# Rounded halves of q and k placed by ScalarE or VectorE, and rows of maxima issued from ScalarE's queue, in a clustered-attention and mixture-of-experts kernel

## The chip, the cores and the metric

One core of one Trainium2 chip runs the whole kernel in one launch. The metric is the device time in microseconds of one execution. A profile is one execution taken by the hardware profiler; its times count from the start of its span.

## The reference

Attention over 4 batches of 8 heads, 768 positions, 64 dimensions. Every query and key is assigned to the nearest of 16 centroids, and a query sees only keys of its own cluster. The result then goes through a routed layer of 8 experts with at most 80 tokens each.

```python
q_assign = np.argmax(np.einsum('bhsd,hcd->bhsc', q_n, c_n), axis=-1)
k_assign = np.argmax(np.einsum('bhsd,hcd->bhsc', k_n, c_n), axis=-1)
mask = q_assign[:, :, :, None] == k_assign[:, :, None, :]
scores = np.where(mask, scale * np.matmul(q, k.transpose(0, 1, 3, 2)), -1000000000.0)
scores = scores - np.max(scores, axis=-1, keepdims=True)
attn = np.exp(scores)
attn = attn / (np.sum(attn, axis=-1, keepdims=True) + 1e-09)
x = np.matmul(attn, v)                        # then merged over heads to 3072 x 512
logits = x @ w_gate                           # top-1 of 8 experts, the 80 largest gates each
out[tok] = gate[tok, None] * (np.maximum(x[tok] @ w1[e], 0.0) @ w2[e])
```

## The kernel before

The 32 heads are worked in 16 pairs. Each head has six units of 128 keys, and a pair has twelve. For each unit TensorE computes two score tiles of 128 x 384 (lines 470 and 471, two matmuls each), ScalarE takes their exponentials (line 476), GpSimd adds them up (line 485), and TensorE multiplies them by the values (line 494).

q and k are split into a rounded half "hi" (type fp32r) and the rest "lo". A head's operands lie in two tiles, QAB and KAB, of 128 partitions x 2 slots x 768; there are six of each, used in turn. Slot 0 holds hi, 16 rows of one-hot cluster numbers and, in QAB, one row with the negative of each query's maximum; slot 1 holds hi and lo stacked. `pair` fills them: ScalarE rounds k and q into a tile `hi` (lines 269 and 295), GpSimd subtracts to get lo (lines 271 and 301), and DMAs on SyncE's queue (SP) carry the parts into place, all through `copy`, so that they all carry line 80 in the profile. KAB gets four DMAs of hi, QAB two that write both slots at once, and each head gets two one-hot DMAs (`oh`) for KAB and two for QAB. Masked q (line 291) needs the one-hot tile and a matmul (line 289) first.

One pair ahead of the scores, the maxima pass runs on slot 0 alone: a matmul (line 433) into one of two PSUM tiles `sm`, and a VectorE maximum over it (line 435). After a head's twelve maxima, `shift` reduces them, TensorE turns them (line 453), ScalarE rounds them into `row` (line 456), and a DMA of 3 KB writes them as one row of QAB. Line 471 cannot run for that head before this row has landed; line 433 cannot run before hi and the one-hot rows are in place. Score tiles have three PSUM buffers.

The order of all instructions is made by a planner (class `Flow`): steps carry an engine, a duration, what they need and a due time `at`, and the planner emits the step that can start first on its engine, in the order of due times among those nearly ready. The table `CFG` holds the due times. Every engine and every DMA queue then runs its own list in that order, so a step that waits holds up all behind it on its engine. A DMA uses one of eight semaphores in turn and waits until the DMA eight places ahead of it in the program has landed, whichever queue that one is on.

After the pairs come the logits, the choice of tokens, and eight experts (lines 1014 and 1042).

Of the kernel before, what the change touches and what calls it, by code (L numbers as in the profile page):

```python
# [7 lines left out]
F32 = mybir.dt.float32  # L8
# [11 lines left out]
CFG = dict(at=dict(sum=-2.92, av=6.36, xT=11.45, lt=5.48, turn=6.25, sm=1.07, exp=-3.24, mx=-0.64), stick=1.99, wait=0.06,  # L20
           idle=0.25, dummy=128, bias=0.67, side=(-1.86, 0.07), prep=(-0.18, 0.32), lead=(-40.37, -29.82, -36.45, -34.77, -18.44),
           zero=(-15.23, 0.59, -7.6, 0.13), start=dict(pe=6.1, act=4.8, dve=7.5, pool=2.5, dma=0.0), warm=48, cold=38.0, lag=0.8,
           hold=dict(dve=(0.08, -0.06), act=(0.67, 0.23), pe=(0.25, 0.02)), nab=6, pps=9, sums=8, xts=4, vs=2, skew=3, raws=4,
           lds=3, keys=1, adds=6, weigh=(8, 5.0, 4.5), slots=(16, 8), native1=(), native2=(0, 1, 2, 3, 4, 5), early=((2, 6),
           185.8), scaled=(), spread=(), mix=dict(ld=-22.86, st=-21.43, hi1=-7.61, lo1=-8.07, hi2=-7.72, lo2=2.21, xg=-34.18,
           xp=-9.37, out=11.74, sc=-9.18, a0=4, a1=2, a2=5, spare=0.3))
# [10 lines left out]
BOTH = ("dve", "pool")  # L37


class Program:  # L40
# [160 lines left out]
    def assign(self, b, p):  # L201
# [34 lines left out]
        yield Step("act", .58, also=("dve", .75), needs=[("hi", "q", *divmod(r - 2, self.NP))] if r > 2 else [])  # L236
# [14 lines left out]
    def pair(self, b, p):  # L251
# [9 lines left out]

        yield Step("none", 0.0, needs=[("ld", "k", b, p)])
# [4 lines left out]
        for f in range(2):  # L267
            yield Step("act", .5)
            nc.scalar.copy(hi[:, f * HS:(f + 1) * HS], t[:, f * HS:(f + 1) * HS])  # L269
# [9 lines left out]
        yield Step("none", 0.0, needs=[("oh", b, p)], key=("hi", "k", b, p), dma=[.1] * 4)  # L279
        onehot("k", self.KAB)  # L280
        yield Step("none", 0.0, needs=[("ld", "q", b, p), ("oh", b, p)])
# [10 lines left out]
        for f in range(2):  # L292
            fs = slice(f * HS, (f + 1) * HS)
            yield Step("act", .5)
            nc.scalar.copy(hi[:, fs], t[:, fs])  # L295
# [116 lines left out]
    def ready(self, b, h, full):  # L412

        p = h // 2
        if b or p:
            return [("full" if full else "hi", n, b, p) for n in "kq"]
        return [["k0l", "q0l", "full0"], ["k1l", "q1l", "q1h", "k1h", "oh1", ("hi", 1)]][h] if full else [[("hi", 0)], ["k1h", "oh1", ("hi", 1)]][h]
# [19 lines left out]
    def shift(self, b, h):  # L437
# [68 lines left out]
    def turns(self, r):  # L506
# [4 lines left out]
        for f in range(2):  # L511
# [4 lines left out]
            yield Step("act", .48, alt=("dve", .55), give="misc", key=("turn", r, f), dma=[1.1])  # L516
# [697 lines left out]
    def prologue(self, flow):  # L1214
# [11 lines left out]
        for p in range(CFG["lds"]):  # L1226
            for n in "kq":
                dma(("ld", n, 0, p), 1.09, self.load, 0, p, n)
# [21 lines left out]
        for r in range(CFG["vs"] - 1):  # L1250
            dma(("ldv", r), 1.09, self.load_v, r)
# [5 lines left out]
    def stream(self, flow):  # L1257
# [10 lines left out]
        def loads(n):  # L1268

            for r in range(CFG["lds"], R):  # L1270
                yield Step("dma", 1.09, needs=self.taken(n, *divmod(r - CFG["lds"], NP)), key=("ld", n, *divmod(r, NP)))
                self.load(*divmod(r, NP), n)

        def vs():
            for r in range(CFG["vs"] - 1, R):
                yield Step("dma", 1.09, needs=[("av", r - CFG["vs"], NC - 1), ("span", r - CFG["vs"])] if r >= CFG["vs"] else [], key=("ldv", r))
                self.load_v(r)

        def begin(t):
# [19 lines left out]
            if k in (4, 10) and 2 * r + k // 6 < self.NT:  # L1299
                i = 2 * r + k // 6  # L1300
                flow.dma(flow.now, .73)
# [29 lines left out]
        def weighs():  # L1331
            N1, K1 = self.w1.shape[1] // P, E * self.w1.shape[1] // P
            for n in range(K1):
                u = CFG["weigh"][0] + int(CFG["weigh"][1] * n)
                e, k = divmod(n, N1)
                yield Step("dma", 1.46, key=("wl", n), late=CFG["weigh"][2], needs=[("st", units[u][0] * NC + units[u][1], 0)] + [("wm", n - 1)] * (n > 0), at=u)
# [120 lines left out]
def Step(eng, t, **more):  # L1457

    return SimpleNamespace(**{**dict(eng=eng, t=t, key=None, needs=(), at=None, late=0.0, rows=.5, early=False, alt=None, also=None, dma=(), take=None, give=None, kind=0, room=None, seq=False, swdge=0.0, port=(), made=None, bar=None, even=False), **more})
# [38 lines left out]
class Flow:  # L1498
# [5 lines left out]
    def __init__(self, free):  # L1504
        self.free, self.end, self.lanes, self.lock = dict(free), {}, [], {}
        self.now, self.kind, self.queue, self.work, self.origin, self.port = 0.0, 0, 0.0, {0: 3000.0, 1: 3100.0}, 0.0, 0.0
        self.idle, self.filled, self.first, self.ahead = None, 0, None, 1e9

# [50 lines left out]
    def run(self):  # L1559
        while True:  # L1560
# [52 lines left out]
            done = start + t  # L1613
# [100 lines left out]
```

## Time and profile before

| | |
|---|---|
| three runs | median 605.52 us, 604.53 to 613.6 |
| the profiled execution | 609.25 us |
| its span, first to last instruction | 607.1 us |
| TensorE busy (matmuls) | 566.0 us, 93% |
| VectorE, GpSimd, ScalarE busy | 416.1, 393.5, 331.3 us |
| mean granted TensorE clock | 0.951 |
| DMA | 124.47 MB, mean 205 GB/s |

The pairs take the span up to about 486 us, the choice of tokens up to about 519 us, the experts the rest. Busy shares of TensorE come from modelled ends of pipelined matmuls, so 93% doesn't say that it worked at its peak; what it waited for is read from its waits. "SPq" in a row is SyncE's queue issuing a DMA, and a DMA in the chain of waits is the time from its issue to its landing.

### The profile page before, as it was taken

Reading aid. Unit: us, or ns where it says so; the run is one execution under the profiler, and the core shown is the slowest. Engines: PE = TensorE matmul, PEld = TensorE weight load, DVE = VectorE, ACT = ScalarE, POOL = GpSimd, SP = SyncE. Lnnn points to the kernel's source line nnn. Section 1 sums busy time; section 2 is a strip of 40 time slices with the busy share of each in tenths; the row PEclk is TensorE's granted clock in tenths of the full one; section 3 lists DMA queues with packets and bytes.
Section 4 is the critical chain, followed back from the end, with each engine's and each line's share of the span. In section 5 each row is a group of like instructions: output and inputs, shape, how many; then the busy total and the mean of one; then the engine's idle time right before and its main releaser. Section 6 shows DMA issues by size and latency. Waiting matters only on the chain.

```text
span 607.1 us, 11292 instructions
## 1 busy us (share of the span) xinstructions
PE 566.0 (93%) x3986; PEld 370.4 (61%) x3986; DVE 416.1 (69%) x815; ACT 331.3 (55%) x704; POOL 393.5 (65%) x226
## 2 busy tenths in 40 slices
PE   7999998998999888989999979999999977899996
PEld 5568565565567465655666556665676457656563
DVE  4866676676577664666876657658777677797872
ACT  7436565565558463664576436555565360554750
POOL 5338696967299694946897928479978121547541
PEclk9558999999999997999999979999999987999999
DMA  7476868786866697688658873855594267799920
GB/s 236 104 178 205 238 180 217 196 235 179 230 178 167 178 239 211 171 231 230 175 152 202 235 237 90 221 134 159 142 375 160 103 216 279 240 391 376 387 100 22
DMA packets 73912, 124.47 MB, mean 205 GB/s; under 512 B 11809, under 2 KB 38977, under 8 KB 73857
## 3 DMA queue, kind: packets, MB, share of 16 engines
q1 hardware_dynamic: 72832, 121.12, 68.0%
q0 software_dynamic: 1024, 2.64, 1.4%
q8 instruction: 31, 0.51, 0.4%
q14 instruction: 25, 0.20, 0.1%
HBM read 70.96 MB, written 13.99 MB: 140 GB/s over the span
## 4 chain that ended last, share of the span: by engine, by line
PE 72%; DMA 11%; issue 5%; SPq 4%; ACT 4%; DVE 3%; POOLq 0%; POOL 0%; ACTq 0%; DVEq 0%
PE av L494 18%; PE sm L433 11%; PE st L470 10%; PE st L471 10%; PE yp L1042 6%; DMA QAB<-row 3%; PE hp L1014 3%; DMA QAB<-oh 3%; SPq L80 3%; DMA out_dram<-room,si 2%; PE misc L532 2%; PE misc L211 1%; PE misc L515 1%; PE misc L289 1%; DMA ldv<-in_v_dram 1%
## 5 line engine op out<-in xcount | busy, mean ns | idle before, releaser
L435 DVE TENSOR_REDUCE mx<-sm 128x1 f32<-128x384 f32 x384 | 203.5, 552 | 87.9 <-PE sm L433 84.6
L485 POOL TENSOR_TENSOR sum<-sum,pp 128x768 f32<-128x768 f32 x122 | 219.5, 1832 | 9.9 <-ACT pp L476 9.5
L476 ACT ACTIVATE pp<-st 128x384 f32<-128x384 f32 x384 | 174.6, 489 | 89.8 <-PE st L471 78.5
L433 PE MATMUL sm<-KAB,QAB 80*128 80x384 f32 x384 | 143.2, 396 | 7.2 <-DMA QAB<-oh 6.2
L494 PE MATMUL av<-pp,ldv 128*64 128x384 f32 x768 | 142.7, 500 | 0.0
L471 PE MATMUL st<-QAB,KAB 81*128 81x384 f32 x384 | 134.0, 349 | 8.2 <-DMA QAB<-row 8.2
L470 PE MATMUL st<-QAB,KAB 128*128 128x384 f32 x384 | 136.7, 356 | 0.0
L485 POOL TENSOR_TENSOR sum<-pp 128x768 f32<-128x768 f32 x32 | 59.4, 1869 | 60.3 <-ACT pp L476 54.2
L433 PEld LDWEIGHTS sm<-KAB,QAB 80*128 80x128 f32 x384 | 74.7, 202 | 30.1 <-issue 12.3
L494 PEld LDWEIGHTS av<-pp,ldv 128*64 128x64 f32 x768 | 48.3, 137 | 63.7 <-issue 61.6
L471 PEld LDWEIGHTS st<-QAB,KAB 81*128 81x128 f32 x384 | 75.7, 197 | 10.0 <-DMA QAB<-row 10.0
L470 PEld LDWEIGHTS st<-QAB,KAB 128*128 128x128 f32 x384 | 75.6, 197 | 5.4 <-issue 4.0
L301 POOL TENSOR_TENSOR ldq<-ldq,hi 128x768 fp32r<-128x768 f32 x15 | 27.6, 1839 | 39.6 <-ACT hi L295 35.7
L1072 POOL DMA_INDIRECT out_dram<-room,si x8 | 25.7, 3212 | 37.8 <-DVE room L1067 28.6
L1340 DVE TENSOR_REDUCE most<-weigh 128x1 f32<-128x1024 f32 x32 | 38.7, 1209 | 3.7 <-DMA weigh<-in_w_dram 3.7
L928 DVE SCALAR_TENSOR_TENSOR w1p<-raw,scales,w1p 128x1024 f16<-128x1024 f32 x29 | 36.1, 1277 | 0.4 <-ACT w1p L917 0.4
L271 POOL TENSOR_TENSOR ldk<-ldk,hi 128x768 fp32r<-128x768 f32 x15 | 27.4, 1828 | 10.6 <-ACT hi L269 7.6
L951 POOL DMA_INDIRECT xg<-xs,gi x8 | 19.9, 2482 | 21.1 <-issue 14.8
L1014 PEld LDWEIGHTS <-w1p 128*128 128x128 f16 x768 | 28.5, 100 | 4.7 <-issue 4.7
L1014 PE MATMUL hp<-xt,w1p 128*128 128x80 f16 x768 | 28.8, 202 | 0.3 <-ACT xt L990 0.3
L917 ACT ACTIVATE w1p<-raw,scales 128x1024 f16<-128x1024 f32 x25 | 27.3, 1143 | 1.3 <-DVE OH L624 1.3
L291 DVE SCALAR_TENSOR_TENSOR ldq<-misc,ldq 128x384 f32<-128x384 f32 x30 | 16.6, 553 | 14.7 <-PE misc L289 13.4
(247 smaller groups left out, 617.9 us busy)
## 6 DMA issues: line engine op xcount, KB each, us to landing
raw<-in_w_dram SPq DMA_DIRECT2D x40, 512.0 KB
weigh<-in_w_dram SPq DMA_DIRECT2D x32, 512.0 KB
KAB<-hi SPq DMA_DIRECT2D x60, 192.0 KB
QAB<-hi SPq DMA_DIRECT2D x30, 384.0 KB
room<-in_w_dram SPq DMA_DIRECT2D x20, 512.0 KB
ldk<-in_kT_dram SPq DMA_DIRECT2D x16, 384.0 KB
ldq<-in_qT_dram SPq DMA_DIRECT2D x16, 384.0 KB
ldv<-in_v_dram SPq DMA_DIRECT2D x16, 384.0 KB
```

What stands on the lines that cost most here:

```text
L301: nc.gpsimd.tensor_tensor(lo, t, hi.bitcast(F32), op=ALU.subtract)
L433: nc.tensor.matmul(s, lhsT=qj, rhs=k[0:D + C, 0, f * HS:(f + 1) * HS], start=True, stop=True)
L435: nc.vector.tensor_reduce(mx[:, j, f:f + 1], s, axis=AX.X, op=ALU.max)
L470: nc.tensor.matmul(s, lhsT=k[:, 1, ks], rhs=q[:, 1, qs], start=True, stop=False)
L471: nc.tensor.matmul(s, lhsT=k[0:D + C + 1, 0, ks], rhs=q[0:D + C + 1, 0, qs], start=False, stop=True)
L476: self.nc.scalar.activation(self.st["pp", g, c][:, f], self.st.pop(("s", g, c, f)), AF.Exp, scale=float(self.D) ** -0.5)
L485: eng.tensor_tensor(flat(t), flat(a), flat(self.st["pp", g, c]), op=ALU.add)
L494: nc.tensor.matmul(a[i * D:(i + 1) * D, f, 0:HS], lhsT=v[:, c, i, :], rhs=st["pp", 2 * r + i, c][:, f], start=(c == 0), stop=(c == NC - 1) ...
L928: nc.vector.scalar_tensor_tensor(t[:, 1], raw, s, t[:, 0], op0=ALU.mult, op1=ALU.subtract)
L1014: nc.tensor.matmul(hp[:, f, :], lhsT=wt[:, a, fs], rhs=xt[:, x, k, :], start=(k == 0 and i == 0), stop=(k == K - 1 and i == 2))
L1042: mm = lambda i, l, r, **kw: nc.tensor.matmul(yp[0:Mb, i], lhsT=l, rhs=r, **{"start": False, "stop": False, **kw})
L1340: nc.vector.tensor_reduce(self.most[:, R + n:R + n + 1], t, axis=AX.X, op=ALU.max, apply_absolute_value=True)
```

## The change

In slot 0 of KAB and QAB, hi is now written by a copy on ScalarE or VectorE (`place`, whichever the planner finds free first) instead of by DMA. The hi part of slot 1 still comes by DMA: one for each head in KAB, and one of 192 KB in QAB, issued with lo after GpSimd's subtraction. The one-hot DMAs of QAB are issued right behind those of KAB, ahead of the masking of q. The row of maxima is issued from ScalarE's queue. The planner has other durations for DMAs, knows of the eight semaphores, and has a new table of due times; with it the order of all engines is made anew, and some copies out of PSUM (`x`, `xT`, `xt`) go to VectorE that ran on ScalarE. The arithmetic is the same.

```diff
-           hold=dict(dve=(0.08, -0.06), act=(0.67, 0.23), pe=(0.25, 0.02)), nab=6, pps=9, sums=8, xts=4, vs=2, skew=3, raws=4,
+           hold=dict(dve=(0.08, 0.02), act=(0.72, 0.03), pe=(0.23, 0.04)), nab=6, pps=9, sums=8, xts=4, vs=2, skew=1, raws=4,
...
+CP, OH, LD, LV, WL = .85, .17, 1.3, 1.6, 2.2
...
+        def place(AB, hi):
+            for i, g in enumerate(pos):
+                yield Step("act", .92, alt=("dve", .62), port=("dve",), needs=free)
+                if flow.which == "act":
+                    nc.scalar.copy(AB[g][0:D, 0, :], hi[i * D:(i + 1) * D, :])
+                else:
+                    nc.vector.tensor_copy(AB[g][0:D, 0, :], hi[i * D:(i + 1) * D, :])
+
         yield Step("none", 0.0, needs=[("ld", "k", b, p)])
...
-        yield Step("pool", 1.82, port=BOTH, needs=free + [("sim", b, p)], early=True, dma=[.55] * 4)
+        yield from halves(hi, t)
+        yield Step("pool", 1.82, port=BOTH, needs=free + [("sim", b, p)], early=True, dma=[CP] * 2)
         nc.gpsimd.tensor_tensor(lo, t, hi.bitcast(F32), op=ALU.subtract)
         for i, g in enumerate(pos):
-            r = slice(i * D, (i + 1) * D)
-            copy(self.KAB[g][0:D, 0, :], hi[r, :])
-            copy(self.KAB[g][D:2 * D, 1, :], hi[r, :])
-        yield Step("none", 0.0, key=("full", "k", b, p), dma=[.55] * 2)
+            copy(self.KAB[g][D:2 * D, 1, :], hi[i * D:(i + 1) * D, :])
+        yield from place(self.KAB, hi)
+        yield Step("none", 0.0, key=("full", "k", b, p), dma=[CP] * 2)
...
-        yield Step("none", 0.0, needs=[("ld", "q", b, p), ("oh", b, p)])
+        yield Step("none", 0.0, needs=[("ld", "q", b, p), ("oh", b, p)], key=("ohq", b, p), dma=[OH] * 4)
+        onehot("q", self.QAB)
...
-        yield Step("none", 0.0, key=("hi", "q", b, p), dma=[1.09] * 2 + [.1] * 4)
-        for i, g in enumerate(pos):
-            copy(self.QAB[g][0:D], hi[i * D:(i + 1) * D].unsqueeze(1).broadcast_to([D, 2, S]))
-        onehot("q", self.QAB)
+        yield from halves(hi, t)
+        yield from place(self.QAB, hi)
+        yield Step("none", 0.0, key=("hi", "q", b, p))
         yield Step("pool", 1.82, port=BOTH)
         nc.gpsimd.tensor_tensor(lo, t, hi.bitcast(F32), op=ALU.subtract)
-        yield Step("none", 0.0, key=("full", "q", b, p), dma=[.55] * 2)
+        yield Step("none", 0.0, key=("full", "q", b, p), dma=[CP] * 4)
+        for i, g in enumerate(pos):
+            copy(self.QAB[g][0:D, 1, :], hi[i * D:(i + 1) * D, :])
...
-        yield Step("act", .25, give="misc", key=("shift", g), late=CFG["lag"], dma=[.06], at=NC * g - NC - 4)
+        yield Step("act", .25, give="misc", at=NC * g - NC - 4)
         row = w.tile([NC, P], F32R, name="row", bufs=2)
         nc.scalar.copy(row, mt)
-        self.copy(q[D + C:D + C + 1, 0, :].rearrange("o (j p) -> o j p", p=P), row)
+        yield Step("act", .8, key=("shift", g), late=CFG["lag"], aside=True, at=NC * g - NC - 4)
+        nc.scalar.dma_start(q[D + C:D + C + 1, 0, :].rearrange("o (j p) -> o j p", p=P).bitcast(F32), row.bitcast(F32))
...
         for t in times:
-            self.queue = max(self.queue, ready) + .6
-            self.free["dma"] = max(self.free["dma"], self.queue + .65) + t
-        return self.free["dma"] + 1.05
+            self.queue = max(self.queue, ready, self.landed.pop(0)) + .6
+            self.free["dma"] = max(self.free["dma"], self.queue + .55) + t
+            self.landed.append(self.free["dma"] + .9)
+        return self.free["dma"] + .9
+
+    def aside(self, start, issue):
+
+        done = max(start, self.landed.pop(0)) + issue
+        self.landed.append(done + 1.4)
+        return done
```

The first place is the row of maxima of the sixth head, whose operands lie in QAB_109. Before, it stands on SP behind a turned output (`xs`), an expert's weights (`weigh`), two lo parts and a block of zeros for the output:

```order
L523 DMA xs<-x 128x3x128 x2
L1338 DMA weigh<-in_w_dram 128x1024
L80 DMA QAB_104<-ldq 64x768
L80 DMA QAB_105<-ldq 64x768
L1302 DMA out_dram<-zero 512x1x128
L80 DMA QAB_109<-row 1x6x128
L193 DMA ldq<-in_qT_dram 128x768
```

In the changed kernel the same row stands on ScalarE, and the row of the head before it, with one of the copies of hi, a little ahead:

```order
L267 CAST hi<-ldq 128x384
L466 CAST row<-misc 6x128
L267 CAST hi<-ldq 128x384
L468 DMA QAB_108<-row 1x6x128
L273 COPY QAB_104<-hi 64x768
L487 ACTIVATE pp<-st 128x384 x10
L466 CAST row<-misc 6x128
L468 DMA QAB_109<-row 1x6x128
L487 ACTIVATE pp<-st 128x384
```

The row is off SP's list, and exponentials (`pp<-st`) now stand behind its DMA on ScalarE.

The second place is where hi and the one-hot rows of q go into QAB_108 and QAB_109 for the ninth pair. Before, on SP, the one-hot rows stand behind both hi DMAs:

```order
L193 DMA ldk<-in_kT_dram 128x768
L80 DMA QAB_106<-row 1x6x128
L1338 DMA weigh<-in_w_dram 128x1024
L80 DMA QAB_108<-hi 64x2x768
L80 DMA QAB_109<-hi 64x2x768
L80 DMA QAB_108<-oh 16x384 x2
L80 DMA QAB_109<-oh 16x384 x2
L523 DMA xs<-x 128x3x128 x2
```

In the changed kernel, on SP for the same pair, they stand behind those of KAB and ahead of everything else:

```order
L81 DMA KAB_114<-oh 16x384 x2
L81 DMA KAB_115<-oh 16x384 x2
L81 DMA QAB_108<-oh 16x384 x2
L81 DMA QAB_109<-oh 16x384 x2
L534 DMA xs<-x 128x3x128
L199 DMA ldv<-in_v_dram 128x768
L194 DMA ldk<-in_kT_dram 128x768
L534 DMA xs<-x 128x3x128
L1349 DMA weigh<-in_w_dram 128x1024
L81 DMA QAB_108<-hi 64x768
L81 DMA QAB_109<-hi 64x768
```

And on ScalarE of the changed kernel the hi halves of that pair are rounded, and the first head's is copied into place; the second head's copy (QAB_109) stands on VectorE:

```order
L267 CAST hi<-ldq 128x384
L466 CAST row<-misc 6x128
L267 CAST hi<-ldq 128x384
L468 DMA QAB_106<-row 1x6x128
L273 COPY QAB_108<-hi 64x768
L487 ACTIVATE pp<-st 128x384 x3
L530 COPY x<-misc 128x384
```

What the maxima pass needs of q is a DMA of small rows that was issued long before, and two copies on an engine.

Counted over the whole program, 33 of the 60 copies of hi stand on ScalarE and 27 on VectorE; 12 copies `x` and 9 copies `xT` moved from ScalarE to VectorE in the pairs, and 7 of 8 copies `xt` in the experts; SP issues 458 DMAs in place of 520 and ScalarE 32 in place of none; GpSimd's list has the same instructions.

## Rows read from the trace of the kernel before

**Rows 1.** The page, chain that ended last, by engine
```profile
PE 72%; DMA 11%; issue 5%; SPq 4%; ACT 4%; DVE 3%; POOLq 0%; POOL 0%; ACTq 0%; DVEq 0%
```
**Rows 2.** Waits of TensorE: who for whom, total us, times, longest us
```profile
PE st L471 <- DMA QAB<-row: 8.2, 5, 3.3
PE sm L433 <- DMA QAB<-oh: 6.2, 4, 3.5
PE misc L289 <- ACT row L456: 2.5, 7, 0.4
PE misc L219 <- ACT row L456: 1.4, 4, 0.3
```
**Rows 3.** Chain that ended last, in order of time: start us, us, what
```profile
89.87 4.96 DMA QAB<-row
...
217.68 0.93 ACT hi L295 x2
...
220.42 0.70 SPq L80
...
221.85 7.16 DMA QAB<-oh
229.10 0.66 PE sm L433
...
354.11 3.25 DMA QAB<-row
...
512.72 3.30 DMA xg<-xs,gi
```
**Rows 4.** Timeline of SyncE's queue, 84 to 95 us: start us, us, what
```profile
87.86 1.16 SPq L80 DMA_DIRECT2D QAB<-ldq  x2
89.06 0.71 SPq L1302 DMA_DIRECT2D out_dram<-zero  x1
89.87 0.77 SPq L80 DMA_DIRECT2D QAB<-row  x1
```
**Rows 5.** Stretches: start:end length, busy us (count) by engine, PEclk, DMA, GB/s
```profile
15.50:49.60 34.10, 32.81 (x120) 23.49 (x121) 24.70 (x56) 15.03 (x32) 14.51 (x8) 0.50 0.66 173
...
227.10:233.90 6.80, 4.80 (x15) 2.66 (x15) 3.17 (x5) 1.94 (x5) 4.78 (x3) 0.50 0.67 177
...
356.80:363.70 6.90, 6.29 (x19) 5.84 (x20) 2.74 (x6) 3.88 (x8) 1.93 (x2) 0.51 0.76 240
...
50.00:450.00 400.00, 379.29 (x2205) 246.62 (x2204) 274.08 (x556) 234.33 (x538) 301.62 (x168) 0.98 0.72 196
```
**Rows 6.** Line 80, issues on SyncE's queue: ns min/median/max, first and last start
```profile
L80 SPq DMA_DIRECT2D QAB<-oh x64: 540/877/1756, 22.5 to 433.3; - x64
...
L80 SPq DMA_DIRECT2D KAB<-hi x60: 467/587/1507, 16.9 to 418.4; - x60
L80 SPq DMA_DIRECT2D QAB<-row x32: 737/762/1278, 28.8 to 457.6; - x32
```
**Rows 7.** Groups by line on ScalarE and VectorE: busy us, mean ns, idle before
```profile
L269 ACT CAST hi<-ldk 128x384 fp32r<-128x384 f32 x30 | 14.6, 513 | 0.0
L502 ACT COPY xT<-av 128x384 f32<-128x384 f32 x32 | 14.3, 479 | 14.3 <-PE av L494 14.1
L519 ACT COPY x<-misc 128x384 f32<-128x384 f32 x29 | 14.0, 481 | 22.8 <-PE misc L515 22.8
L938 ACT CAST w2p<-raw 128x1024 fp32r<-128x1024 f32 x2 | 2.1, 1050 | 0.0
L521 DVE COPY x<-misc 128x384 f32<-128x384 f32 x3 | 1.7, 551 | 4.0 <-PE misc L515 4.0
L940 DVE CAST w2p<-raw 128x1024 fp32r<-128x1024 f32 x1 | 0.7, 694 | 2.1 <-PE hp L1014 2.1
```
**Rows 8.** Line 485, the sums on GpSimd and VectorE: ns min/median/max
```profile
L485 POOL TENSOR_TENSOR sum<-pp x32: 1812/1824/3188, 43.0 to 467.8; 128x768 f32<-128x768 f32 x32
L485 DVE TENSOR_TENSOR sum<-sum,pp x6: 945/956/2373, 471.7 to 479.9; 128x768 f32<-128x768 f32 x6
```

More of the change, by code (lines that the diff above doesn't have):

```diff
@@ L19 @@
 BASE = 0x3C000000
[L20 to L26 removed]
+CFG = dict(at=dict(sum=-2.92, av=6.67, xT=9.63, lt=2.68, turn=5.95, sm=1.01, exp=-3.28, mx=-1.52), stick=1.83, wait=0.06,
+           idle=0.25, dummy=128, bias=-0.01, side=(-1.52, -0.09), prep=(-0.18, 0.07), lead=(-38.46, -29.9, -37.8, -34.77, -18.17),
+           zero=(-15.24, 0.52, -5.03, 0.13), start=dict(pe=6.1, act=4.8, dve=7.5, pool=2.5, dma=0.0), warm=48, cold=38.0, lag=0.4,
+           hold=dict(dve=(0.08, 0.02), act=(0.72, 0.03), pe=(0.23, 0.04)), nab=6, pps=9, sums=8, xts=4, vs=2, skew=1, raws=4,
+           lds=3, keys=1, adds=6, weigh=(8, 5.1, 1.5), slots=(19, 5), native1=(), native2=(0, 1, 2, 3, 4, 5), early=((2, 6),
+           185.8), scaled=(), spread=(), mix=dict(ld=-22.86, st=-21.43, hi1=-7.76, lo1=-13.16, hi2=-7.72, lo2=2.21, xg=-34.18,
+           xp=-9.37, out=9.27, sc=-9.18, a0=4, a1=4, a2=5, spare=0.35))
 SWITCH = {(0, 1): .01, (1, 0): .01, (0, 2): .108, (1, 2): .108, (2, 0): .16, (2, 1): .196, (0, 0): 0.0, (1, 1): 0.0, (2, 2): 0.0}
@@ L235, in assign @@
         nc.tensor.matmul(fi[:, 0:HS], lhsT=self.tie, rhs=es, start=True, stop=True)
-        yield Step("act", .58, also=("dve", .75), needs=[("hi", "q", *divmod(r - 2, self.NP))] if r > 2 else [])
+        yield Step("act", .58, also=("dve", .75), needs=[("ohq", *divmod(r - 2, self.NP))] if r > 2 else [])
         oh = st["oh", b, p] = w.tile([P, HS], F32R, name="oh", bufs=2)
@@ L260, in onehot, with halves @@
                 self.onehot(AB[g], self.st["oh", b, p], n == "q", i)
+        def halves(hi, t):
+            for f in range(2):
+                fs = slice(f * HS, (f + 1) * HS)
+                yield Step("act", .5)
+                nc.scalar.copy(hi[:, fs], t[:, fs])
+        def place(AB, hi):
[5 more added lines that the diff above has]
+                    nc.vector.tensor_copy(AB[g][0:D, 0, :], hi[i * D:(i + 1) * D, :])
         yield Step("none", 0.0, needs=[("ld", "k", b, p)])
@@ L1270, in loads @@
             for r in range(CFG["lds"], R):
-                yield Step("dma", 1.09, needs=self.taken(n, *divmod(r - CFG["lds"], NP)), key=("ld", n, *divmod(r, NP)))
+                yield Step("dma", LD, needs=self.taken(n, *divmod(r - CFG["lds"], NP)), key=("ld", n, *divmod(r, NP)))
                 self.load(*divmod(r, NP), n)
@@ L1275, in vs @@
             for r in range(CFG["vs"] - 1, R):
-                yield Step("dma", 1.09, needs=[("av", r - CFG["vs"], NC - 1), ("span", r - CFG["vs"])] if r >= CFG["vs"] else [], key=("ldv", r))
+                yield Step("dma", LV, needs=[("av", r - CFG["vs"], NC - 1), ("span", r - CFG["vs"])] if r >= CFG["vs"] else [], key=("ldv", r))
                 self.load_v(r)
@@ L1457, in Step @@
 def Step(eng, t, **more):
-    return SimpleNamespace(**{**dict(eng=eng, t=t, key=None, needs=(), at=None, late=0.0, rows=.5, early=False, alt=None, also=None, dma=(), take=None, give=None, kind=0, room=None, seq=False, swdge=0.0, port=(), made=None, bar=None, even=False), **more})
+    return SimpleNamespace(**{**dict(eng=eng, t=t, key=None, needs=(), at=None, late=0.0, rows=.5, early=False, alt=None, also=None, dma=(), take=None, give=None, kind=0, room=None, seq=False, swdge=0.0, port=(), made=None, bar=None, even=False, aside=False), **more})
 class Lane:
@@ L1507, in __init__ @@
         self.idle, self.filled, self.first, self.ahead = None, 0, None, 1e9
+        self.landed = [0.0] * 8
     def add(self, *lanes):
@@ L1612, in run @@
                 self.kind = step.kind
-            done = start + t
+            done = self.aside(start, t) if step.aside else start + t
             if eng == "dma":
```

23 lines of the change are left out of this document (8 added, 15 removed).

## The prediction

> **What bounds the kernel now.** I read the page first. In the chain that ended last TensorE holds 72%, DMA 11% and SyncE's queue 4% [rows 1], so the kernel is mostly TensorE's work, with some 15% of the chain on transfers and their issue. The change takes no matmul of the pairs away, so it can win only what TensorE loses to waiting. A share of the chain is not such a loss, because TensorE may do other work beside a link of it. So I read TensorE's own waits next: 8.2 us in 5 waits for the row of maxima and 6.2 us in 4 waits for the one-hot rows of q [rows 2]. All other waits there are far smaller; those for ScalarE's `row`, which gives a PSUM bank back, are 2.5 + 1.4 us. Then I read the chain in order of time for how such a wait arises, and the clock by stretches.
>
> A row lands late because of what stands ahead of it. At 89.87 us SP issues one behind two lo parts of 192 KB and a 256 KB block of zeros [rows 4], and it lands 4.96 us later [rows 3] though it has 3 KB. The one-hot rows of q lie at the end of a longer path: ScalarE rounds hi from 217.68 us, SP issues two hi DMAs from 220.42 us, the one-hot DMA goes out at 221.85 us and lands 7.16 us later, and the maxima matmul starts at 229.10 us [rows 3], 11.4 us after the rounding began.
>
> Two of the waits also cost clock. From 227.10 to 233.90 us and from 356.80 to 363.70 us the granted clock is 0.50 and 0.51 [rows 5], the 1.2 GHz level; the first stretch begins inside the wait that ends at 229.10 us, the second inside the one behind the row issued at 354.11 us, which lands at 357.36 us [rows 3].
>
> **The change part by part.** First what it removes.
>
> Row: on ScalarE's queue nothing of SP stands ahead of it, so neither SP's list nor, as I take it, SP's backlog of transfers delays it. The five waits go: 8.2 us. From below, if it lands as late as now, nothing is won.
>
> One-hot rows and hi: hi no longer travels, and the one-hot rows go out before q is even masked. From rounding to the first maxima matmul there remain the rounding (0.93 us [rows 3]) and two copies, about 3 us in place of 11.4. The four waits go: 6.2 us. Late next is VectorE's maximum, which the plan paces anyway.
>
> Clock: without these waits the two stretches run at 2.4 GHz. Half of 6.8 + 6.9 us is 6.8 us. Together 8.2 + 6.2 + 6.8 = 21.2 us, the most that the trace shows to be had here.
>
> Now what it adds.
>
> ScalarE: a copy of 64 x 768 is not in the trace. Between 513 ns for 384 elements and 1050 ns for 1024 [rows 7] a straight line gives 835 ns, and 33 of them 27.6 us. A row's issue took 762 ns on SP [rows 6]; 32 of them on ScalarE, taken as equally long, 24.4 us. The 12 copies `x` at 481 ns and 9 copies `xT` at 479 ns that leave it [rows 7] give back 10.1 us. The sum is 41.9 us. From 50 to 450 us ScalarE was busy 234.3 of 400 us [rows 5], so most of this lies beside TensorE's work; with that cover gone it would cost all 41.9 us. What shows of ScalarE on TensorE now is 3.9 us [rows 2]. Some 36 of the 41.9 us fall in those 400, so ScalarE's idle time there drops from 166 to about 129 us; with busy time over idle time as the measure, waits grow by half, to 6 us. Two things are worse than before: up to 3 us of rounding, issue and copying now stand together, and three score buffers cover about 1 us. Bounds: 0 (the work only adds, so no gain) and 41.9 us; I take 4, near the row that shows such waits.
>
> The row's issue also waits for a semaphore: it must find the DMA eight places ahead of it landed, and while it waits every exponential behind it waits, and TensorE's scores with them. On SP the same wait held up only DMAs. I count it as zero while SP is no more than two or three DMAs behind, and come back to it below.
>
> VectorE: 27 copies. A cast of 1024 took 694 ns [rows 7], so 768 take about 520 ns, 14.1 us; 21 copies out of PSUM at 551 ns [rows 7] are 11.6 us. That is 25.7 us where it was busy 274.1 of 400 [rows 5]. A second cost comes from GpSimd. The sums of line 485 show it: on GpSimd most take 1.82 us and one took 3.19; on VectorE, where both operands are in SBUF, the median is 0.96 us and one took 2.37 [rows 8]. Each long one is longer by about 1.4 us, as if it had waited for the other engine. If every copy waited out a whole GpSimd sum, that would be 27 x 1.83 = 49 us of VectorE; the plan starts such copies at the end of a sum, so I take 2 us on TensorE, between 0 and 49.
>
> On this the Trainium skill ("SBUF — State Buffer", Who interferes with whom) says that a VectorE copy in its two-port mode and a GpSimd instruction exclude each other for the whole instruction. The long sums agree with such a wait. By the rule alone, with GpSimd busy three quarters of the time, copies started at random would wait some 18 us in all on VectorE, still inside its idle time.
>
> SP: 30 hi DMAs of 587 ns and 32 rows of 762 ns leave its list [rows 6], 42 us of queue time, and 60 copies of 192 KB (30 out of KAB's, 30 halves of QAB's) leave the DMA engines. I count nothing for that: it only makes what is left arrive sooner.
>
> Residual: in the new order some heads have as little matmul work between the row's transposition and its first use as the tightest had before, and the row needs about 0.25 us of rounding, 0.76 us of issue and a landing. I take 2 us over all heads, between 0 and the present 8.2.
>
> Experts and choice of tokens: `xt` moves to VectorE, weights are loaded in another order, matmuls are the same. Zero, plus or minus 2 us.
>
> Sum: 609.25 - 21.2 + 4 + 2 + 2 = 596.05 us in terms of the profiled execution, whose span is 607.1 us with 2.15 us around it. The median of the runs is 605.52 us, 0.6% below it; in its terms the forecast is 592.4 us.
>
> **The rivals.** *Waits change their names.* The row is on another queue but shares the DMA engines with SP's transfers, and lands as late as now. Then 8.2 us and the second clock stretch (3.4 us) stay, and 21.2 - 11.6 = 9.6 us is won, less the 6 us on ScalarE and VectorE: 605.6, or 602 us in terms of the median. For it: the engines are busy 0.72 of the time from 50 to 450 us [rows 5], and the new order leaves rows somewhat less room. Against it: a gather issued from GpSimd's queue, 80 rows of 2 KB, landed 3.30 us after issue [rows 3] beside weight loads on SP.
>
> The Trainium skill ("DMA: Bandwidth & Descriptors", Issuing engines are not separate DMA queues) speaks for this rival: DMAs from different engines run on the same 16 DMA engines and interleave, and another issuer saves only the time to issue. By that rule the row would still share bandwidth with SP's backlog, and the result would be nearer to 602 us. The gather above doesn't decide it.
>
> *ScalarE's queue becomes the bound.* Each row's issue holds the queue for h us, its 0.76 us and the wait for its semaphore. Beyond the 1.1 us that three score buffers cover, TensorE waits too. If the 32 issues hold it for 2.1 us on average, this costs 32 x 1.0 = 32 us, and 609.25 - 21.2 + 32 + 4 = 624 us, or about 620 in terms of the median: slower. It breaks even near h = 1.65 us, a semaphore wait of 0.9 us on average. For it: landings of 5 to 7 us occur on SP [rows 3], and eight places are about 6 us of issues. Against it: SP has 62 issues fewer.
>
> *The start gains too.* From 15.50 to 49.60 us the clock is 0.50 [rows 5], and the new order brings the first value matmuls and the second head's scores a little earlier. If the clock rose some 14 us sooner, another 6.8 us go: about 585 us. Nothing in the trace says that it will.
>
> **How the numbers follow.** Forecast 0.52, at 592.4 us, its own range 586 to 598; waits renamed 0.24, at 602; ScalarE's queue 0.14, at 620; start gains 0.10, at 585. About 2% is what a measurement of this kernel can tell from no change; that is 593.4 us and 617.6 us. The forecast lies on the lower edge: I give 0.31 of its 0.52 to faster and 0.21 to the same. With the start's 0.10 and 0.01 of the renamed waits faster is 0.42; the same is 0.21 + 0.23 = 0.44; slower is 0.14. The range 583 to 609 holds the first two cases nearly whole and most of the start's; it leaves out the slow one, the only one above 609.
>
> **What would show it.** Right: TensorE's waits name `row` and `oh` for under 3 us together, no stretch at the 1.2 GHz level between 60 and 480 us, the row landing about 2 us after its issue, and ScalarE some 35 us busier from 50 to 450 us. Wrong: rows on ScalarE's queue that take 3 us or more; exponentials whose idle time ends with a DMA or with ScalarE's own issue of a row; VectorE copies of hi of more than 1 us; or a lasting drop of the clock in the pairs.

## The result: slower by 1.25%, and the profile after

Over twenty runs each, the changed kernel's median is 617.87 us (613.18 to 627.79), the kernel before's 609.88 us. The ratio is 1.0125, 95% interval 1.009 to 1.016: 7.6 us slower, where I forecast 13 us faster. The profiled execution of the changed kernel took 625.89 us (span 623.4), one of its longer ones; where a time matters below, it is a ratio of many runs, and the profile only says where to look; shorter executions below show the same two waits.

TensorE's waits in the changed kernel, against [rows 2] (who waits for whom: total us, times, longest us):

```profile
PE sm L443 <- DVE mx L445: 10.6, 5, 4.7
PE st L482 <- DMA QAB<-row: 10.1, 7, 2.7
...
PE misc L245 <- DVE zh L243: 2.5, 7, 0.7
PE misc L220 <- ACT row L466: 2.4, 7, 0.3
```

The wait for the one-hot rows is gone, as forecast. The wait for the row is not: 10.1 us in place of 8.2. And there is a new one: the maxima matmuls wait 10.6 us for VectorE's maximum, to free their PSUM tile. The longest of these, on TensorE, VectorE and GpSimd (start us, us, what; in brackets the idle time before and its releaser), each from the timeline of its engine:

```profile
86.37 0.69 PE L443 MATMUL sm<-KAB,QAB 80*128 80x384 f32 x1 [4.67 <-DVE mx L445]
```
```profile
79.52 0.55 DVE L532 COPY x<-misc 128x384 f32<-128x384 f32 x1
80.10 5.76 DVE L275 CAST QAB<-hi 64x768 fp32r<-64x768 f32 x1
85.77 1.01 DVE L445 TENSOR_REDUCE mx<-sm 128x1 f32<-128x384 f32 x2
```
```profile
80.09 1.83 POOL L309 TENSOR_TENSOR ldq<-ldq,hi 128x768 fp32r<-128x768 f32 x1
81.89 3.55 POOL L496 TENSOR_TENSOR sum<-sum,pp 128x768 f32<-128x768 f32 x2
```

VectorE's copy of hi begins 0.01 us after GpSimd's subtraction and lasts 5.76 us. It is over 0.42 us after the last of three GpSimd instructions that follow one another without a gap; meanwhile the maxima stand behind it. Over all 27 copies on VectorE (line 275: ns min/median/max, first and last start):

```profile
L275 DVE CAST KAB<-hi x17: 540/555/1993, 46.2 to 426.9; 64x768 fp32r<-64x768 f32 x17
L275 DVE CAST QAB<-hi x10: 551/2044/5756, 52.8 to 398.1; 64x768 fp32r<-64x768 f32 x10
```

Undisturbed, a copy takes 0.55 us (I had worked out 0.52); those into QAB have a median of 2.04. Sixteen of the 27 take 0.54 to 0.56 us, and all of them begin while GpSimd runs nothing. The other eleven begin while it runs an instruction and take more than 1 us, and each of the eleven ends 0.41 or 0.42 us after the end of an instruction on GpSimd (worked out from the trace): nine behind the first that ended, the two longest behind three. The second longest, and the same copy in a second profile of this kernel (the first run below):

```profile
199.25 4.79 DVE L275 CAST QAB<-hi 64x768 fp32r<-64x768 f32 x1
```
```profile
200.67 1.23 DVE L275 CAST QAB<-hi 64x768 fp32r<-64x768 f32 x1
201.44 2.15 POOL L309 TENSOR_TENSOR ldq<-ldq,hi 128x768 fp32r<-128x768 f32 x1
```

There it got in behind the first instruction, though the next one began without a gap, and that one took 2.15 us where it took 1.80 before. Which of the two happens is left open.

The row, in the chain that ended last, and the DMAs that SP had issued by then:

```profile
380.83 0.26 ACT row L466
381.11 5.66 DMA QAB<-row
386.81 0.44 PE st L482
```
```profile
379.02 0.58 SPq L1349 DMA_DIRECT2D weigh<-in_w_dram  x1
380.15 1.11 SPq L81 DMA_DIRECT2D KAB<-hi  x2
```

ScalarE issues it 0.02 us after the rounding has ended, and still it lands 5.66 us later: 512 KB of weights and two parts of hi were issued by SP in the two us before it. Over all 32 rows (worked out from the trace's landings) the delay from rounding to issue fell from 1.11 to 0.03 us in the mean, and the time from issue to landing rose from 2.84 to 3.23.

Some stretches at half clock (columns as in [rows 5]):

```profile
84.50:91.30 6.80, 4.93 (x15) 4.93 (x16) 4.87 (x8) 1.97 (x4) 3.50 (x3) 0.50 0.59 160
203.90:210.70 6.80, 6.13 (x20) 5.94 (x20) 4.59 (x10) 2.46 (x5) 3.07 (x2) 0.50 0.81 239
...
449.70:456.50 6.80, 6.80 (x23) 6.80 (x22) 4.12 (x8) 3.83 (x9) 4.50 (x3) 0.50 0.92 361
```

The first begins inside the wait that ends at 86.37 us, the second inside another wait for the maxima, 3.61 us long, which ends at 204.57. The stretches of before at 227 and 357 us [rows 5] are gone, others stand in their place.

### The profile page after: what moved, and what is told of

Its sections match the earlier page's. It is cut to its first block, busy times and chain, and to the rows that moved or that the text cites. A ratio compares the mean times of both kernels' runs of the same rounds, so it can differ in the third digit from the quotient of the medians.

```text
span 623.4 us, 11318 instructions
## 1 busy us (share of the span) xinstructions
PE 574.8 (92%) x3999; PEld 377.7 (61%) x3999; DVE 465.9 (75%) x868; ACT 347.7 (56%) x711; POOL 387.2 (62%) x226
## 3 DMA queue, kind: packets, MB, share of 16 engines
q0 software_dynamic: 1024, 2.64, 1.3%
## 4 chain that ended last, share of the span: by engine, by line
PE 27%; DMA 13%; issue 6%; POOL 2%; DVE 1%; ACT 1%; POOLq 0%; DVEq 0%
DMA out_dram<-room,si 9%; PE av L505 8%; PE st L482 5%; PE st L481 5%; PE sm L443 4%; DMA QAB<-row 4%; POOL xg L962 1%; PE misc L526 1%; PE tot L1435 1%; PE sm L543 1%; PE misc L543 1%; PE misc L212 1%; DMA xg<-xs,gi 1%; PE misc L302 0%; PE q L712 0%
## 5 line engine op out<-in xcount | busy, mean ns | idle before, releaser
L443 PE MATMUL sm<-KAB,QAB 80*128 80x384 f32 x384 | 141.9, 403 | 10.8 <-DVE mx L445 10.6
L482 PE MATMUL st<-QAB,KAB 81*128 81x384 f32 x384 | 136.0, 354 | 10.1 <-DMA QAB<-row 10.1
L505 PE MATMUL av<-pp,ldv 128*64 128x384 f32 x768 | 144.5, 503 | 0.5 <-DVE ne L248 0.5
L481 PE MATMUL st<-QAB,KAB 128*128 128x384 f32 x384 | 138.9, 362 | 0.0
L443 PEld LDWEIGHTS sm<-KAB,QAB 80*128 80x128 f32 x384 | 75.1, 207 | 40.7 <-DVE mx L445 20.5
L1083 POOL DMA_INDIRECT out_dram<-room,si x8 | 20.5, 2562 | 46.6 <-DVE room L1078 43.7
L1025 PEld LDWEIGHTS <-w1p 128*128 128x128 f16 x768 | 30.7, 104 | 4.0 <-issue 4.0
L1025 PE MATMUL hp<-xt,w1p 128*128 128x80 f16 x768 | 31.1, 208 | 0.0
L939 DVE SCALAR_TENSOR_TENSOR w1p<-raw,scales,w1p 128x1024 f16<-128x1024 f32 x24 | 30.0, 1276 | 0.0
L962 POOL DMA_INDIRECT xg<-xs,gi x8 | 17.3, 2160 | 19.9 <-issue 11.5
L928 ACT ACTIVATE w1p<-raw,scales 128x1024 f16<-128x1024 f32 x21 | 23.4, 1143 | 6.1 <-DMA raw<-in_w_dram 4.4
L1053 PE MATMUL yp<-room,hh 128*80 128x512 f32 x52 | 23.7, 597 | 0.0
```

The lines of the kernel that those rows point to most:

```text
L443: nc.tensor.matmul(s, lhsT=qj, rhs=k[0:D + C, 0, f * HS:(f + 1) * HS], start=True, stop=True)
L481: nc.tensor.matmul(s, lhsT=k[:, 1, ks], rhs=q[:, 1, qs], start=True, stop=False)
L482: nc.tensor.matmul(s, lhsT=k[0:D + C + 1, 0, ks], rhs=q[0:D + C + 1, 0, qs], start=False, stop=True)
L505: nc.tensor.matmul(a[i * D:(i + 1) * D, f, 0:HS], lhsT=v[:, c, i, :], rhs=st["pp", 2 * r + i, c][:, f], start=(c == 0), stop=(c == NC - 1) ...
L939: nc.vector.scalar_tensor_tensor(t[:, 1], raw, s, t[:, 0], op0=ALU.mult, op1=ALU.subtract)
L1025: nc.tensor.matmul(hp[:, f, :], lhsT=wt[:, a, fs], rhs=xt[:, x, k, :], start=(k == 0 and i == 0), stop=(k == K - 1 and i == 2))
```

## The experiments

All but one keep the order of the program as it is on every engine (the planner runs with the old numbers, and only the instruction that it places is another, or goes to another queue; in some kernels made from the one before, the one-hot DMAs of q also stand earlier on SP, as their edits show). So each differs from a neighbour by one thing, or by edits that were measured one at a time as well. Ratios are to the kernel before, measured beside it, with 95% intervals.

**The changed kernel again, and its two suspects one at a time**

> The changed kernel once more, for a second profile beside the runs that follow. Every theory: 1.0 to 1.02 times before; TensorE's waits name the maxima on VectorE (10.6 us in the first profile) and the row (10.1 us).

Measured: 1.0103 (1.0012 to 1.0195); waits of 12.4 us for the row, 7.0 us for the maxima. The two losses are there again; the maxima are 3.6 us less, the second long wait of the first profile.

```diff
-                    nc.vector.tensor_copy(AB[g][0:D, 0, :], hi[i * D:(i + 1) * D, :])
+                    nc.vector.tensor_reduce(out=AB[g][0:D, 0, :], in_=hi[i * D:(i + 1) * D, :].unsqueeze(2), axis=AX.X, op=ALU.max)
```

> The changed kernel in the same order of instructions on every engine; the 27 copies of hi on VectorE are written as a maximum over an axis of length 1, which gives the same values. Theory 1 (a VectorE copy of hi is held while GpSimd's sums run): none of the 27 takes over 1.3 us (in the changed kernel one took 5.76 and one 4.79), though each takes longer than 0.55 us when nothing disturbs it, about 0.9; TensorE's wait for the maxima falls from 10.6 to under 2 us, the stretches at half clock behind the two long waits go, and the time falls by 10 to 17 us, to 0.985 to 0.995 of before. Theory 2 (VectorE simply has too much work): the copies together take about as long as now, 24 against 36 us, but TensorE's wait for the maxima stays at 6 us or more and the time stays within 5 us of the changed kernel's.

Measured: 1.0007 (0.9956 to 1.0057). Line 275 now (same view as above):

```profile
L275 DVE TENSOR_REDUCE KAB<-hi x17: 933/935/948, 46.3 to 416.4; 64x768 fp32r<-64x768 f32 x17
L275 DVE TENSOR_REDUCE QAB<-hi x10: 933/947/949, 55.6 to 387.9; 64x768 fp32r<-64x768 f32 x10
```

None takes over 0.95 us, beside the same sums, and the wait for the maxima is down to 0.3 us; the wait for the row stays, 10.3 us in 8. So theory 1 holds: the copies were held, and VectorE's work as such, 25 us in these copies, delays nothing that shows. The time fell less than expected (1.2% from 1.0125, not 2 to 3).

```diff
-                    nc.vector.tensor_copy(AB[g][0:D, 0, :], hi[i * D:(i + 1) * D, :])
+                    nc.scalar.copy(AB[g][0:D, 0, :], hi[i * D:(i + 1) * D, :])
```

> The changed kernel with the 27 copies of hi on VectorE issued on ScalarE instead, at the same place of the program; every other instruction in the same order on its engine. Theory 1 (VectorE copies are held by GpSimd): TensorE's wait for the maxima falls under 2 us; ScalarE has 22 us more, of which a few show as waits of TensorE for its exponentials: 0.99 to 1.00 of before. Theory 2 (too much work on VectorE): the same fall. Theory 3 (ScalarE is the bound, my rival of ScalarE's queue): slower than the changed kernel by 5 us or more, with TensorE's waits naming ScalarE.

Measured: 1.0015 (0.9962 to 1.0068). The wait for the maxima is down to 0.3 us here too, and the one for exponentials that has come in its place is 0.4 us: 22 us more on ScalarE hardly show. Theory 3 falls.

```diff
-        nc.scalar.dma_start(q[D + C:D + C + 1, 0, :].rearrange(
+        nc.sync.dma_start(q[D + C:D + C + 1, 0, :].rearrange(
```

> The changed kernel with the row's DMA issued from SP's queue again, at the same place of the program; every other instruction in the same order on its engine. Theory A (the row is late because its transfer shares the DMA engines with SP's transfers, whoever issues it): the time from the rounding of the row to its landing is longer by the queue's delay alone, 3.3 us in the mean growing to 4 to 5, the row's wait on TensorE stays between 8 and 16 us, and the time between -2 and +8 us of the changed kernel's. Theory B (ScalarE's queue is what makes rows late or exponentials wait): the wait for the row falls under 5 us and the time by 5 us or more. Theory C (ScalarE's queue saves what was planned): the wait for the row grows beyond 20 us and the time by over 12 us.

Measured: 1.0031 (0.9967 to 1.0095), the wait for the maxima as it was, the wait for the row smaller:

```profile
PE sm L443 <- DVE mx L445: 7.0, 4, 4.7
PE st L482 <- DMA QAB<-row: 4.5, 5, 1.5
```

Back on SP's queue the row comes sooner: the delay of its issue is 0.38 us in the mean, the landing 2.58 (3.37 in the changed kernel's second profile). Theory B has the size right: ScalarE's queue was the loss. Theory A's forecast for this run failed (its 8 to 16 us of waits), but its grounds say how the queue loses. I count each of SP's transfers whole, from its issue to its landing. In the second profile 794 KB of them were under way when a row was issued (mean of 32), and 186 KB of these stand behind the row in the program: SP had run on past it. With the row in SP's list SP cannot, and 638 KB were under way. Issue by issue, the row's landing goes with these bytes (correlation 0.79 and 0.68). So do the means of all sixteen profiles of this study, 2.45 to 3.48 us with 479 to 947 KB (correlation 0.88); about the straight line through them, rows from ScalarE's queue land 0.09 us later in the mean than rows from SP's.

**Do the bytes make the row late?**

```diff
-                nc.sync.dma_start(t, self.w1[e, k * P:(k + 1) * P, :])
+                nc.sync.dma_start(t[:, 0:P], self.w1[e, k * P:(k + 1) * P, 0:P])
```

> The changed kernel in the same order; each of the 32 loads weigh brings 128 of its 1024 columns (64 KB in place of 512), and VectorE's maximum reads these 128 columns eight times, so that it is as long as before. What it leaves out: seven eighths of the weights in the maximum that scales the experts' weights. Theory A (a row lands late by what is under way on the DMA engines when it is issued, whoever issues it): with 14.7 MB less in the pairs the row's landing falls from 3.4 us in the mean to 2.7 or less, TensorE's waits for it from 12 to under 7 us, and the time by 4 to 9 us against the changed kernel. Theory B (the row is late for a reason of ScalarE's queue that doesn't hang on the bytes under way): the landing stays at 3.2 us or more and the waits over 9 us.

Measured: landing 2.54 us in the mean, 479 KB under way, with the row still on ScalarE's queue. TensorE's waits:

```profile
PE sm L443 <- DVE mx L445: 10.6, 5, 4.7
PE st L482 <- DMA QAB<-row: 4.7, 4, 1.9
```

Theory A of this run holds: with fewer bytes under way the same queue brings the row sooner, and a queue matters by what it lets pass. The bytes don't fix a single landing: one row of the changed kernel landed in 1.75 us with 1024 KB under way. The time, 1.0042 (1.0000 to 1.0084), carries the wait for the maxima as before.

The Trainium skill ("DMA: Bandwidth & Descriptors", Issuing engines are not separate DMA queues) says that DMAs from different engines share the 16 DMA engines. That was the ground of my rival of waits that change their names, and the trace agrees; that leaving SP's list also lifts a brake on SP's later transfers is told by these runs alone.

**Both edits to the changed kernel**

> The changed kernel in the same order, with both edits: the 27 copies of hi on VectorE as a maximum over an axis of length 1, and the row's DMA on SP's queue. If the two losses are separate (copies held by GpSimd, 7 to 11 us of waits and the half clock behind them; the row on ScalarE's queue, some 8 us), they add: waits for the maxima under 1 us, for the row under 6 us, 595 to 602 us, 0.98 to 0.99 of before. If they are one loss seen at two places (TensorE waits for something else as soon as one is gone), the time stays at 604 us or more, within 3 us of the better of the two single edits.

> The run with both edits to the changed kernel in its own order, once more: 0.977 to 0.992 of before if the first measurement holds.

Measured: 0.9844 (0.9767 to 0.9921), and the second time 0.9863 (0.9824 to 0.9903), 600.15 and 604.17 us. The two losses add; the waits are 3.6 and 5.3 us for the row and none for the maxima.

```diff
-                yield Step("act", .92, alt=("dve", .62), port=("dve",), needs=free)
+                yield Step("act", .92, alt=("dve", .95), needs=free)
```

> The changed kernel with the copies of hi on VectorE as a maximum over an axis of length 1 and the row on SP's queue, and with the planner told of both (0.95 us on VectorE, free of GpSimd's port; the row's DMA as the kernel before plans it); the due times are the changed kernel's, so the order is made anew. If the order of the changed kernel was good and only the two costs were wrong, within 3 us of the run that keeps the order, 597 to 603 us; if due times fitted to other costs matter more, 604 us or more.

(With the two edits above, and the row planned as the kernel before plans it.) Measured: 0.9968 (0.9927 to 1.0009), 609.19 us. Better numbers for two steps gave a worse order: the pairs end no later (the last exponential at 466.3 us, in the two runs above at 468.2 and 471.8, though half clock at the start lasts 20.5 us here and 37.5 there), and in the experts TensorE waits for ScalarE's `hh`:

```profile
PE yp L1052 <- ACT hh L1033: 8.1, 2, 6.9
```

It looks as if the due times belong to the costs that they were found with; no other table was tried.

**Parts of the change in the order of the kernel before**

```diff
-        self.copy(q[D + C:D + C + 1, 0, :].rearrange("o (j p) -> o j p", p=P), row)
+        nc.scalar.dma_start(q[D + C:D + C + 1, 0, :].rearrange("o (j p) -> o j p", p=P).bitcast(F32), row.bitcast(F32))
```

> The kernel before in its own order, with the row's DMA on ScalarE's queue alone. My prediction: the five waits for the row and one of the half-clock stretches go, 8 to 12 us, less up to 4 on ScalarE: 0.985 to 0.993 of before. The theory from the runs so far (SP runs on while the row is on another queue, so that more bytes are ahead of it): the delay of the issue, 1.1 us in the mean, goes, the landing grows from 2.8 to 3.2 us or more, the waits for the row stay between 5 and 12 us, and the time is 0.995 to 1.010 of before.

Measured: 1.0080 (1.0024 to 1.0136). TensorE's waits, against [rows 2]:

```profile
PE sm L433 <- DMA QAB<-oh: 11.5, 6, 4.1
PE st L471 <- DMA QAB<-row: 3.1, 3, 1.9
```

5.1 us of the row's waits went, as I had forecast, and 5.3 came for the one-hot rows. A wait has changed its name. The two sums balance, so they don't account for the 0.8%. The stretches at half clock between 50 and 450 us are 20.5 us long in place of 13.7, which is 3.4 us of time; the rest is open. That the rows, gone from SP's list, no longer hold back the weights and hi that stand ahead of the one-hot rows there is argued, not shown, by this run.

```diff
         onehot("k", self.KAB)
+        onehot("q", self.QAB)
...
-        onehot("q", self.QAB)
```

> The kernel before in its own order, with the one-hot DMAs of QAB issued right behind those of KAB alone. My prediction's term for the one-hot rows: TensorE's wait for them, 6.2 us in 4, goes, and with it one half-clock stretch of 3.4 us, 0.985 to 0.99 of before. Rival: the DMAs of hi into QAB, issued at the same place and 384 KB each, are late next, and TensorE's wait for QAB's hi takes over 4 us or more: within 3 us of before.

Measured: 0.9985 (0.9931 to 1.0038): nothing, the rival. No wait names the one-hot rows, but TensorE still stands until 228.61 us, where it stood until 229.10 before:

```profile
222.19 1.39 SPq L80 DMA_DIRECT2D QAB<-hi  x2
```
```profile
228.61 0.66 PE L433 MATMUL sm<-KAB,QAB 80*128 80x384 f32 x1 [4.06 <-issue]
```

The first hi DMA, issued at 222.19 us, lands 6.22 us later, at 228.41. "Issue" is a wait that the profile could not name; here it was hi.

```diff
-            copy(self.KAB[g][0:D, 0, :], hi[r, :])
+            nc.scalar.copy(self.KAB[g][0:D, 0, :], hi[r, :])
...
-            copy(self.QAB[g][0:D], hi[i * D:(i + 1) * D].unsqueeze(1).broadcast_to([D, 2, S]))
+            nc.scalar.copy(self.QAB[g][0:D, 0, :], hi[i * D:(i + 1) * D])
+            copy(self.QAB[g][0:D, 1, :], hi[i * D:(i + 1) * D])
```

> The kernel before in its own order, with the one-hot DMAs of QAB ahead and with slot 0 of KAB and QAB written by 60 copies on ScalarE, at the places where the DMAs of hi were issued; the row stays on SP's queue, and QAB gets 192 KB of hi for slot 1 in place of 384. In the run with the one-hot rows alone TensorE waited until 228.6 us for hi, whose DMA had been issued at 222.2 us. If that transfer is what was left, the waits of the maxima pass for DMAs (6.2 us in the kernel before) go, with the half-clock stretches behind them, and of the 50 us of copies on ScalarE a few show: 0.98 to 0.99 of before. If the copies hold the exponentials, TensorE waits for ScalarE for over 5 us more than before, and the time is 0.995 to 1.01 of before.

Measured: 0.9674 (0.9615 to 0.9733), 592.12 us, the fastest kernel of the study. Its longest waits on TensorE, and two stretches:

```profile
PE q L702 <- DVE dug L648: 2.7, 1, 2.7
PE misc L219 <- ACT row L457: 2.7, 5, 1.3
PE st L471 <- ACT pp L477: 2.7, 4, 0.9
```
```profile
17.10:37.60 20.50, 19.14 (x72) 11.80 (x71) 15.12 (x36) 11.82 (x22) 8.04 (x5) 0.50 0.48 120
50.00:450.00 400.00, 389.19 (x2293) 251.18 (x2290) 283.05 (x563) 280.40 (x609) 314.96 (x176) 1.00 0.63 179
```

No wait names the DMA of `row` or of `oh`, and no stretch at half clock is left between 50 and 450 us: 2293 matmuls in these 400 us, 2205 before [rows 5]. The 50 us of copies on ScalarE show as 2.7 us of waits for exponentials. The row is on SP's queue and no longer late, with 30 DMAs of 192 KB fewer and 30 halved: it lands 3.29 us after its rounding in the mean, 3.95 before.

**What is left: the order, and the two suspects in the old order**

> The changed kernel in its own order, with all 60 copies of hi on ScalarE and the row on SP's queue: the same three edits as the run of the kernel before with one-hot rows ahead and copies on ScalarE (592 us), in the other order. If the new due times cost nothing by themselves, 590 to 597 us, 0.965 to 0.975 of before. If the new order is the third loss (later experts, tighter rows), it stays where the run with both edits stands, 599 to 605 us, 0.98 to 0.99.

(The changed kernel with both edits shown above, copies on ScalarE and row on SP.) Measured: 0.9863 (0.9796 to 0.9929), 602.65 us. The same three edits cost 1.9% more in the new order. There the row is late again:

```profile
PE st L482 <- DMA QAB<-row: 9.4, 6, 2.7
```

It takes no longer from rounding to landing than in the old order (3.23 us in the mean, 3.29 there); it has less room. Between the matmul that turns a head's maxima and the first matmul that needs the row, TensorE is busy for 4.7 us (median over the heads) in the new order and 5.7 in the old one; it is under 5 us for 19 of the 32 heads there and for 11 here. That this room is what the order costs is argued from the 9.4 us of waits; it was not tried by itself, and of the 15.8 us between the two profiles 5.1 are a longer half clock at the start (30.8 us in place of 20.5).

> The kernel before in its own order with one-hot rows ahead and 60 copies on ScalarE, and now also with the row on ScalarE's queue: only this differs from the run at 592 us. If the queue is a loss in any order (SP runs on past the row, the row's landing grows by 0.5 us or more), TensorE's wait for the row grows from under 2 to 5 us or more and the time by 4 to 12 us, to 0.975 to 0.987 of before. If it was a loss only in the new order, the time stays within 3 us of 592, 0.963 to 0.972.

(The fastest kernel with the row's DMA as two experiments above.) Measured: 0.9814 (0.9752 to 0.9875), 599.31 us: 1.4% more, the size expected, by another way than expected. The row isn't late here (no wait names its DMA); ScalarE is:

```profile
PE st L471 <- ACT pp L477: 5.2, 9, 1.2
...
PE tp L986 <- ACT room L965: 2.6, 1, 2.6
...
PE misc L516 <- ACT x L520: 2.2, 2, 1.1
```

These three were 2.7, 1.0 and 0.5 us without the row on ScalarE. The first and the third grew by 4.2 us, and seven of their eleven waits end within 4 us of a row's issue; that is my rival of ScalarE's queue, with 0.68 us of issue and no wait for a semaphore behind it. The second falls at 509.7 us, after the last row. And half clock at the start lasts 30.8 us in place of 20.5, which is 5.1 of the 11.6 us between the two profiles; no run shows that the row's queue did this.

```diff
-            nc.scalar.copy(self.QAB[g][0:D, 0, :], hi[i * D:(i + 1) * D])
+            nc.vector.tensor_copy(self.QAB[g][0:D, 0, :], hi[i * D:(i + 1) * D])
```

> The kernel before in its own order with one-hot rows ahead, KAB's 30 copies on ScalarE and QAB's 30 on VectorE, as plain copies, at the same places; the row on SP's queue. If a VectorE copy is held while GpSimd's sums follow one another, whatever the order, some of the 30 take 2 to 6 us, TensorE's wait for the maxima is 5 us or more, and the time is 6 to 20 us above the run at 592 us. If only the new order put copies beside sums, all 30 take under 1.3 us and the time is within 4 us of it.

Measured: 1.0185 (1.0119 to 1.0251), 620.43 us: thirty copies on VectorE cost 5.1% of before, some 31 us. The copies, and TensorE's wait:

```profile
L299 DVE CAST QAB<-hi x30: 542/1460/6387, 31.9 to 434.6; 64x768 fp32r<-64x768 f32 x30
```
```profile
PE sm L434 <- DVE mx L436: 16.4, 12, 6.5
```

The new order starts its plain copies with regard to GpSimd's work, the old one doesn't; so the new order limited this loss and did not remove it.

## Why the prediction was wrong, point by point

617.87 us lies above the whole range. The one rival that gave such a time, ScalarE's queue held by semaphores (620 us), is not what happened: the changed kernel has two losses, VectorE's copies and the row on ScalarE's queue, that I had priced at 2 us and at nothing, and an order that costs far more than the 2 us I gave it. Of the signs of being wrong that I named, two came: rows that take 3 us or more, and copies of more than 1 us. Read as a ladder, each step one difference between two measured kernels:

| from | to | ratio to before |
|---|---|---|
| before | one-hot rows ahead, slot 0 by ScalarE | 0.9674 |
| | the new order in place of the old | 0.9863 |
| | row from ScalarE's queue | 1.0015 |
| | 27 of the copies as plain copies on VectorE | 1.0125 |

- **One-hot rows, hi and the clock: the waits go, as forecast, but the size came by a term that I had put at nothing.** The first step of the ladder gives 20 us (0.0326 x 610). For these parts alone I had 6.2 us and half of one stretch, 3.4, less up to 4 on ScalarE. The row's wait of 8.2 us and the second stretch went as well, with the row still on SP's queue. I had booked them on ScalarE's queue, and of the copies that leave the DMA engines I wrote "I count nothing for that". That these did it is argued from the row's landing, 3.29 us after its rounding in place of 3.95; no run takes them away alone. Further, this kernel's profile, 19.5 us shorter, leaves half clock at 37.6 us where the kernel before does at 49.6; half of the 13.6 us fewer spent there is 6.8 us that I had put into a rival. Over the sixteen profiles the half clock at the start lasts 20.5 to 37.5 us, and what sets it is not shown. Without these 6.8 us the step is 12.7 us.
- **The row: this step failed.** I wrote that "neither SP's list nor, as I take it, SP's backlog of transfers delays it". The backlog does, and it is larger than with the row on SP (794 KB under way in place of 638), since SP runs on past a row that it no longer carries. It is my rival of waits that change their names, as to where the row is late. I let the gather's 3.30 us [rows 3] speak against it, and it was no evidence: the rows too landed in 3.23 us in the mean, later than on SP. The price is 1.4 to 1.5% in three pairs of kernels (0.9674 to 0.9814, 0.9863 to 1.0015, 0.9863 to 1.0007, the last with the maximum over one element), and 0.8 to 0.9% in two more (1 to 1.0080, 1.0031 to 1.0125). In the order of the kernel before, the row itself did come sooner (3.18 us after its rounding in place of 3.95), and the loss stood at the one-hot rows or on ScalarE.
- **ScalarE: right in work, right in what shows in the new order.** A copy took 0.829 us (0.835 estimated), an issue 0.68 (0.76 on SP); each of the 32 issues began within 0.04 us of the rounding's end, so the wait for a semaphore was zero, as counted. In the changed kernel ScalarE's exponentials were not waited for.
- **VectorE's copies: mis-sized.** I took 2 us between 0 and 49, because the plan starts such copies at the end of a sum. They cost 1.1%, some 7 us: the 27 copies took 36.3 us where 15 were due, and TensorE waited 10.6 us and lost clock behind it. Two things were wrong: eleven copies did begin while an instruction ran on GpSimd, and two of them were held through three instructions that follow without a gap, not through one. The Trainium skill ("SBUF — State Buffer", Who interferes with whom) has the instruction of either engine hold the other for its whole length. I had worked out 18 us on VectorE from that, the trace shows 21; but three instructions in a row, 5.76 us, are more than one whole length. It was these two copies, and not the sum, that TensorE's two long waits stood behind.
- **Residual, 2 us: too small.** The new order costs 1.9%, some 11 us, with the row's room down from 5.7 to 4.7 us. I had seen that some heads had as little room as the tightest before, and priced it at 2 us. Which of the planner's new numbers takes the room was not tried.

## What to carry to other kernels

Before you move a small, urgent transfer to another queue, count what the old queue will now issue ahead of it: its place in the list was also a brake. A VectorE copy between SBUF tiles beside a busy GpSimd can cost an unbroken run of GpSimd's instructions, and not only its own length; a form that is slower alone but never held, or ScalarE, was cheaper here. When a change bundles a good part with a new plan, put the part alone into the old order first: here it was worth 3.3%, and the rest took 4.5% back.

## What was not expected of the hardware

- A plain VectorE copy of 64 x 768 between SBUF tiles took 0.54 us alone and up to 6.39 us beside GpSimd; a maximum over an axis of one element, on the same tiles, took 0.93 to 0.95 us in all 27 cases. The longest copies were held through three or more GpSimd instructions, most long ones through one.
- A 3 KB transfer landed between 1.74 and 7.28 us after its issue, on a queue that held nothing else.
- The row on ScalarE's queue cost about the same, 1.4 to 1.5%, in two orders, once as a late row and once as late exponentials with a longer start at half clock. Why the two come to the same size is left open.
